# A planner's duration for leaving narrow products, and a new order from it, in a linear attention and MoE kernel

## The chip, the cores and the metric

One Trainium2 chip, one core of it. The metric is the device time of one execution in microseconds (us). The kernel before took 662.56 us (median of 3 runs, 660.89 to 663.44).

## The reference: what is computed

Two layers, one after the other. The first is a complex-valued linear attention over 4 batches, 8 heads, 768 steps and a head dimension of 48. Each step decays a 48 by 48 state by a normalised complex factor, adds an outer product and reads the state:

```
mag = sqrt(a_re*a_re + a_im*a_im);  scale = min(mag, 0.999) / (mag + 1e-6)
for t in range(S):
    S_re, S_im = ar*S_re - ai*S_im + kv(t), ar*S_im + ai*S_re
    y[:, :, t] = einsum('bhd,bhde->bhe', q[:, :, t], S_re)
```

The second takes y as 3072 tokens of 384 numbers through a two-layer network: `gelu(x @ w_in) @ w_out`, with 2048 hidden units and weights that arrive as 64-bit floats.

## The kernel before, in words

**Lanes.** The decay factors are turned into running products. The sequence is cut into four groups of chunks (GROUPS, two of 64 steps and two of 128, each with a mirrored second half), and each group into 4 or 8 slices of 8 rows. `tick` (line 703) does one slice: it normalises the factors of a later slice, runs the scan of this one (`scan`, line 666: for each row a 192-column multiply and a 96-column add on VectorE, each dependent on the last), and turns keys and queries by the products (`towards`, `against`, line 645). What comes out is stored to a buffer in DRAM (tile kq) and loaded again as kqn by the units. `ending` (line 681) and a last `squares_b` and `logs` close a group. In the profile lanes work is a, tab, bt, tt, xt.

**Weights.** 32 pieces (`weights`, line 502), each a 384 KB load into raw, four VectorE instructions on raw, wh, wi_lo or wo_lo, some ScalarE instructions and three TensorE products that split each weight into a high and a low part (wi_hi, wi_lo, wo_hi, wo_lo).

**Units.** 24 units of 128 tokens (`unit`, line 786). Each loads keys, queries and values, turns keys and queries, makes scores (tile kp), outputs and the update of the state st. Its products of at most 64 output rows are called narrow: att<-kp,vn, att<-qT,st, att<-vn,kqn or att<-vn,raw in the profile. The first eight units hold two chunks, the others one. In the latter the narrow products are made `together`, as one step that nothing can be put into.

**Blocks.** 9 blocks of two or three units (`block`, line 1044). For each of 16 pieces of the hidden dimension a block makes the first product (ph<-xT,wi), Gelu on ScalarE twice, a subtraction on VectorE, and the second product (po<-wo), each as three products of high and low parts.

**The order of all work.** Nothing is issued when these functions run. They only hand steps to a planner (class Plan), which knows for each step its engine or engines, its cost and what it must come after. `natural` (line 274) gives each step a starting rank: the length of the longest path behind it, with the scan's VectorE chain weighted by WL, plus a number for its kind from MORE (lanes0 to lanes3, weights, units, blocks). `forward` (line 292) then plays the program through: on each engine, of the steps that are ready, the one of highest rank goes next; on TensorE a step of the same form as the last is preferred where its rank is within STAY, 1.0, of the best. Where a step can go to more than one engine, it goes where its end plus that engine's BIAS is least. `backward` (line 376) plays the plan from its end, and its times are the ranks of the next `forward`. After PASSES, 4, of these the plan with the shortest estimate is kept (`order`, line 406) and issued (`issue`, line 420). The lines of the profile therefore name the place of issue, line 429, for nearly everything; the tiles tell the work apart.

In `forward` TensorE's form of products (narrow, turn, round, full) costs time at a change, and nothing else depends on it:

```
if e == "tensor":
    if start - free[e] > COLD:
        warm = start + WARM
    if start < warm:
        cost *= 2
    if s.form != form:
        cost += ENTER.get(s.form, 0.0) + LEAVE.get(form, 0.0)
    form = s.form
```

Of the kernel before, what the change touches and what calls it, by code (L numbers as in the profile page):

```python
# [79 lines left out]

ROUND, PASS = 0.462e-3, 0.4219e-3

ENTER, LEAVE = dict(narrow=0.09), dict(narrow=0.2, turn=0.075)
STAY = 1.0
COLD, WARM = 3.0, 4.0
TABLES = {AF.Ln: "natural_log_exp_and_others", AF.Exp: "natural_log_exp_and_others", AF.Gelu: "gelu"}
# [8 lines left out]
EARLIER, N_RAW, N_KP = 1, 4, 2  # L95
PASSES = 4
N_A = 4
WL = 4.532

MORE = dict(lanes0=483.83, lanes1=-1595.06, lanes2=-3639.85, lanes3=-3453.18, weights=-1624.01, units=-66.21, blocks=-85.66)  # L100
BIAS = dict(vector=-0.82, scalar=-1.94, gpsimd=0.93, sync=-6.23)


class Step:
# [8 lines left out]
class Plan:  # L113
# [160 lines left out]
    def natural(self):  # L274
# [4 lines left out]
        for i in range(len(steps) - 1, -1, -1):  # L279
# [9 lines left out]
            rest[i] = t  # L289
        return [t + MORE[s.kind] for t, s in zip(rest, steps)]  # L290

    def forward(self, rank):
# [14 lines left out]
        while len(order) < len(steps):  # L307
            best = None
            for e, waiting in pool.items():
# [8 lines left out]
                if len(steps[i].options) > 1:  # L318
                    ends = {o: max(free[o], ready[i], port[other[o]] if o in steps[i].port else 0.0) + c + BIAS[o] for o, (_, c) in steps[i].options.items()}
                    if ends[e] > min(ends.values()) + 1e-9:  # L320
# [119 lines left out]
def lanes_and_chunks(ctx, tc, flags, a_lanes, x_lanes, v_units, w_in, w_out, out):  # L440
# [650 lines left out]
    def ticks(g):  # L1091
        P.chain["vector"] = "lanes", WL
        with P.work(f"lanes{g}"):
            for s in range(end):
                if slices[s][0] == g:
                    tick(s)
        P.chain.pop("vector")
# [255 lines left out]
```

## Time and profile before

| what | value |
|---|---|
| median of 3 runs | 662.56 us |
| lowest and highest run | 660.89, 663.44 us |
| profiled execution, first to last instruction | 659.6 us |
| the profiled span below the median of the runs | 3.0 us |
| TensorE busy | 614.1 us, 93% |
| VectorE busy | 484.1 us, 73% |
| ScalarE busy | 434.1 us, 66% |
| GpSimd busy | 26.1 us, 4% |
| granted TensorE clock, mean | 0.973 |

The profile has one execution, whose span is given from its first to its last instruction; a time of its own beside the span is not given, so the span is set against the median of the runs, 3.0 us above it. In the rows, PE is TensorE, PEld its loading of weights, DVE VectorE, ACT ScalarE, POOL GpSimd and SPq the queue of SyncE, which issues the transfers. A product of two 32-bit operands is two instructions of PE, so counts of such products are twice those of the code. A start-to-start time in the timeline is the time that a run of instructions took up; the second number in a row is its duration, which overlaps the next.

### The profile page before, as it was taken

The numbers are of one execution on the slowest core, as the hardware profiler recorded it, in microseconds if no ns is written. First come the engines' busy times: TensorE is split into PE (matmuls) and PEld (weight loads), VectorE is DVE, ScalarE is ACT, GpSimd is POOL, SyncE is SP. The second block draws the span as 40 slices with busy tenths as digits, with TensorE's granted clock in tenths as the row PEclk, the third lists the DMA queues.
The fourth block names the chain that finished last, engine by engine and source line by source line (L and its number), as shares of the span: only waits on it lengthen the run. The fifth ranks groups of instructions, "written<-read, shape, count | busy, mean of one in ns | idle before, by whom it ended". The sixth has DMA issues, their size and how long they took to land.

```text
span 659.6 us, 13997 instructions
## 1 busy us (share of the span) xinstructions
PE 614.1 (93%) x5154; PEld 563.8 (85%) x5154; DVE 484.1 (73%) x1204; ACT 434.1 (66%) x1107; POOL 26.1 (4%) x74
## 2 busy tenths in 40 slices
PE   4655499999999999999999999999999999999995
PEld 2322277988789999999999999999999999999995
DVE  6999999999999999999989999656334424232211
ACT  8976699999998979787476997535442422232332
POOL 1000100002000000120000000020000000000000
PEclk9787699999999999999999999999999999999999
DMA  9366876668266456687889966487444132110000
GB/s 322 119 158 161 256 225 212 185 196 258 71 197 173 116 135 177 163 173 158 198 198 219 230 157 166 116 167 169 104 88 88 50 64 46 34 51 15 25 1 27
DMA packets 210442, 93.51 MB, mean 142 GB/s; under 512 B 167744, under 2 KB 202688, under 8 KB 210368
## 3 DMA queue, kind: packets, MB, share of 16 engines
q1 hardware_dynamic: 210368, 92.57, 54.6%
q8 instruction: 41, 0.67, 0.4%
q14 instruction: 33, 0.27, 0.1%
HBM read 63.11 MB, written 25.69 MB: 135 GB/s over the span
## 4 chain that ended last, share of the span: by engine, by line
PE 70%; ACT 9%; DVE 9%; issue 2%; DMA 1%; SPq 0%; DVEq 0%; ACTq 0%
PE po L429 27%; PE ph L429 26%; PE att L429 17%; DVE a L429 2%; ACT a L429 1%; DVE tt L429 1%; ACT tab L429 1%; ACT L429 1%; ACT L427 1%; DVE xt L429 1%; ACT gh L429 1%; DVE bt L429 1%; ACT gf L429 1%; DMA raw<-in_w_pieces_dram 1%; ACT square L429 1%
## 5 line engine op out<-in xcount | busy, mean ns | idle before, releaser
L429 PE MATMUL ph<-xT,wi_hi 128*128 128x384 f32 (+1 forms) x864 | 209.2, 324 | 0.0
L429 DVE TENSOR_TENSOR gl<-gf,gh 128x384 fp32r<-128x384 f32 (+1 forms) x144 | 73.7, 512 | 126.4 <-ACT gf L429 126.0
L429 ACT ACTIVATE gh<-ph 128x384 fp32r<-128x384 f32 (+1 forms) x144 | 65.8, 457 | 149.6 <-PE ph L429 149.2
L429 PEld LDWEIGHTS ph<-xT,wi_hi 128*128 128x128 f32 x864 | 154.3, 188 | 2.2 <-ACT gf L429 0.2
L429 PE MATMUL ph<-xT,wi_lo 128*128 128x384 f32 (+1 forms) x432 | 137.3, 318 | 0.0
L429 PE MATMUL po<-wo_hi,gh 128*128 128x384 f32 x384 | 132.5, 345 | 0.9 <-ACT gh L429 0.7
L429 PE MATMUL po<-wo_lo,gh 128*128 128x384 f32 x384 | 129.7, 338 | 0.0
L429 PE MATMUL po<-wo_hi,gl 128*128 128x384 f32 x384 | 92.5, 342 | 0.0
L429 PEld LDWEIGHTS ph<-xT,wi_lo 128*128 128x128 f32 x432 | 81.3, 188 | 0.1
L429 PEld LDWEIGHTS po<-wo_hi,gh 128*128 128x128 f32 x384 | 72.1, 188 | 3.0 <-ACT gh L429 2.0
L429 PEld LDWEIGHTS po<-wo_lo,gh 128*128 128x128 f32 x384 | 72.5, 189 | 0.0
L429 DVE TENSOR_TENSOR tt<-bt,a 128x192 f32<-128x192 f32 x192 | 67.3, 350 | 0.5
L429 PEld LDWEIGHTS po<-wo_hi,gl 128*128 128x128 f32 x384 | 65.9, 188 | 1.6 <-DVE gl L429 0.7
L429 ACT ACTIVATE gf<-ph 128x384 f32<-128x384 f32 (+1 forms) x144 | 65.4, 454 | 2.5 <-DVE gl L429 2.5
L429 DVE TENSOR_TENSOR bt<-tt 128x96 f32<-128x96 f32 x192 | 48.1, 250 | 0.5
L429 PEld LDWEIGHTS att<-qT,kp 96*64 96x64 f32 (+1 forms) x512 | 39.4, 165 | 2.4 <-issue 1.5
L429 PE MATMUL att<-qT,kp 96*64 96x64 f32 (+1 forms) x512 | 41.0, 250 | 0.0
L429 DVE TENSOR_TENSOR kp<-att,causal 128x512 f32<-128x512 f32 x40 | 27.5, 687 | 9.5 <-PE att L429 9.4
L429 ACT ACTIVATE a<-tab 128x384 f32<-128x384 f32 (+1 forms) x48 | 25.6, 534 | 9.3 <-DVE tab L429 9.2
L429 PE MATMUL po<-wh,ident_r 128*128 128x384 f32 x48 | 22.0, 541 | 9.4 <-DVE wh L429 9.3
L429 PE MATMUL att<-tab,ident_r 128*128 128x384 f32 (+1 forms) x20 | 14.8, 896 | 13.6 <-ACT tab L429 13.6
L429 ACT ACT_TABLE_LOAD x21 | 26.9, 1283 | 0.3
(154 smaller groups left out, 992.9 us busy)
## 6 DMA issues: line engine op xcount, KB each, us to landing
kqn<-kq SPq DMA_DIRECT2D x96, 128.0 KB, 3.2
xt<-in_x_lanes_dram SPq DMA_DIRECT2D x24, 384.0 KB, 4.4
kq<-xt SPq DMA_DIRECT2D x48, 192.0 KB, 3.5
a<-in_a_lanes_dram SPq DMA_DIRECT2D x20, 384.0 KB, 3.4
raw<-in_w_pieces_dram SPq DMA_DIRECT2D x16, 384.0 KB, 4.1
raw<-in_moe_w_out_dram SPq DMA_DIRECT2D x16, 384.0 KB, 4.3
vn<-in_v_units_dram SPq DMA_DIRECT2D x24, 256.0 KB, 3.7
kqn<-kq SPq DMA_DIRECT2D x8, 768.0 KB, 5.7
```

The costliest lines, as they stand in the source:

```text
L427: self.nc.scalar.preload_act_table_set(table)
L429: getattr(getattr(self.nc, engine), name)(*args, **kw)
```

## The change

It changes constants of the planner alone: the duration of leaving narrow products, from 0.2 to 0.09 us, the weight WL, the starting ranks MORE and the preferences BIAS. The whole diff:

```
-ENTER, LEAVE = dict(narrow=0.09), dict(narrow=0.2, turn=0.075)
+ENTER, LEAVE = dict(narrow=0.09), dict(narrow=0.09, turn=0.075)
-WL = 4.532
-
-MORE = dict(lanes0=483.83, lanes1=-1595.06, lanes2=-3639.85, lanes3=-3453.18, weights=-1624.01, units=-66.21, blocks=-85.66)
-BIAS = dict(vector=-0.82, scalar=-1.94, gpsimd=0.93, sync=-6.23)
+WL = 4.540
+
+MORE = dict(lanes0=761.48, lanes1=-1519.43, lanes2=-3262.61, lanes3=-8069.14, weights=-1596.23, units=892.75, blocks=-477.53)
+BIAS = dict(vector=-2.11, scalar=-3.87, gpsimd=8.66, sync=-6.23)
```

No step is added or removed; the order of the steps on each engine, and the engine of those that have a choice, come out of the planner anew.

## Rows read from the trace of the kernel before

**Rows 1.** The page: span, busy time, and PE and its granted clock in 40 slices

```profile
span 659.6 us, 13997 instructions
...
PE 614.1 (93%) x5154; PEld 563.8 (85%) x5154; DVE 484.1 (73%) x1204; ACT 434.1 (66%) x1107; POOL 26.1 (4%) x74
...
PE   4655499999999999999999999999999999999995
...
PEclk9787699999999999999999999999999999999999
```

**Rows 2.** Windows: stretch, length, busy us (x instructions) by engine, clock, DMA share, GB/s

```profile
66.00:82.50 16.50, 8.20 (x15) 3.96 (x14) 16.26 (x45) 11.52 (x28) 2.69 (x5) 0.63 0.88 256
...
82.50:260.00 177.50, 176.93 (x2005) 155.52 (x2004) 172.31 (x466) 164.86 (x418) 6.46 (x15) 1.00 0.61 175
260.00:640.00 380.00, 379.56 (x2972) 372.80 (x2971) 235.80 (x533) 200.21 (x518) 13.25 (x26) 1.00 0.52 119
```

**Rows 3.** Groups of DVE from 0 to 60.2 us: the weights' instructions

```profile
L429 DVE SCALAR_TENSOR_TENSOR wh<-raw,wh 128x384 uint32<-128x384 uint32 x10 | 5.5, 554 | 0.1
...
L429 DVE TENSOR_SCALAR wh<-raw 128x384 uint32<-128x384 uint32 x11 | 3.9, 354 | 0.0
L429 DVE TENSOR_SCALAR raw<-wh 128x384 uint32<-128x384 uint32 x10 | 3.6, 357 | 0.1
...
L429 DVE SCALAR_TENSOR_TENSOR wi_lo<-raw 128x384 fp32r<-128x384 uint32 x5 | 2.8, 554 | 0.0
L429 DVE SCALAR_TENSOR_TENSOR wo_lo<-raw 128x384 fp32r<-128x384 uint32 x4 | 2.2, 554 | 0.0
```

**Rows 4.** Timeline of DVE, ACT and SP from 60 to 76 us: start, duration

```profile
60.23 0.25 DVE L429 TENSOR_TENSOR bt<-tt 128x96 f32<-128x96 f32 x1
...
61.17 0.58 ACT L429 ACTIVATE tab<-att,by_partition 128x384 f32<-128x384 f32 x1 [2.67 <-PE att L429]
...
63.26 0.84 ACT L429 ACTIVATE a<-bt 128x768 f32<-128x768 f32 x1
...
70.48 2.62 SPq L429 DMA_DIRECT2D kq<-xt  x3
...
75.78 1.01 SPq L429 DMA_DIRECT2D kqn<-kq  x2
```

**Rows 5.** Timeline of PE around the first narrow runs and around the last

```profile
84.80 1.14 PE L429 MATMUL ph<-vn,kqn 64*64 64x48 f32 x32
85.86 0.75 PE L429 MATMUL att<-ident_r,kqn 128*96 128x128 f32 x8
...
87.61 0.67 PE L429 MATMUL ph<-vn,kqn 64*64 64x48 f32 x16
88.21 0.75 PE L429 MATMUL att<-ident_r,kqn 128*96 128x128 f32 x8
...
599.76 0.34 PE L429 MATMUL po<-wo_hi,gh 128*128 128x384 f32 x1
599.93 0.34 PE L429 MATMUL po<-wo_lo,gh 128*128 128x384 f32 x1
600.20 1.09 PE L429 MATMUL att<-kp,vn 128*64 128x128 f32 x16
...
602.10 0.50 PE L429 MATMUL ph<-xT,wi_hi 128*128 128x256 f32 x2
```

**Rows 6.** Waits of PE's weight loads, 82.5 to 260 us: total us, times, longest

```profile
PEld po L429 <- DVE gl L429: 0.7, 2, 0.6
PEld po L429 <- ACT gh L429: 0.7, 1, 0.7
...
PEld att L429 <- ACT qT L429: 0.5, 1, 0.5
...
PEld att L429 <- ACT kp L429: 0.2, 1, 0.2
```

**Rows 7.** Groups of POOL: the one step on the state

```profile
L429 POOL TENSOR_TENSOR st<-st,m 96x384 f32<-96x384 f32 x1 | 1.0, 1010 | 45.7 <-ACT st L429 45.7
```

## Prediction

> **What bounds the kernel now.** I read the page first, for the span and for the shape of TensorE's (PE's) use: PE is busy for 614.1 us of 659.6, and its slices show two kinds of time, four or five poor slices at the front and a solid row of nines behind [rows 1]. Then the windows by stage. From 66 to 82.5 us PE is busy for 8.20 us of 16.50 at a granted clock of 0.63, which is a mixture of its two levels, 1.2 and 2.4 GHz, after long idle gaps; from 82.5 to 260 us it is busy for 176.93 of 177.50 at full clock, and from 260 to 640 for 379.56 of 380.00 [rows 2]. So the kernel is a prologue of 82.5 us that VectorE (DVE) and ScalarE (ACT) set, and then some 560 us in which PE always has something in hand. In that long part the total of PE's work is fixed, and an order can only change how often PE changes the form of its products and how long it stands between two of them. DVE is busy for 172.31 us of the 177.50 that follow the prologue [rows 2], so in that stretch too whatever DVE does first decides what PE can be given.
>
> The prologue I read in the timeline. The first group of lanes has its last scan step at 60.23 us. Its square on ACT begins at 63.26, because ACT first does work of the second group from 61.17 on; the rows to be stored leave SyncE's (SP's) queue from 70.48, the first unit's load is issued at 75.78 [rows 4], and the first narrow products run at 84.80 [rows 5]. Before 60.2 us DVE also prepares weights: ten pieces, in five groups of instructions whose busy times add up to 5.5 + 3.9 + 3.6 + 2.8 + 2.2 = 18.0 us, so 1.8 us a piece [rows 3].
>
> **The edit to the duration.** It adds and removes no instruction. The number is only added to the planner's own clock when PE goes from narrow products to another form; the choice among ready steps looks at the rank and at STAY, never at this number. In PE's timeline 41 runs of narrow products end, the first at 85.86 us and the last at 602.10 [rows 5], 25 of them before 250 us. What leaving costs the chip can be read there. A run of 32 takes 1.06 us until the next form starts, two runs of 16 take 0.60 each: 2 x 0.60 - 1.06 = 0.14 us for one end more. Entering shows before a run: the step from one 384-column product to the next takes 0.17 us, the one from such a product into a narrow run 0.27, so 0.10 [rows 5]. A visit to narrow products thus costs about 0.24 us beyond its products. The old plan charged 0.09 + 0.20 = 0.29, the new one charges 0.09 + 0.09 = 0.18. **The plan's PE clock goes from 41 x 0.05 = 2.1 us too slow to 41 x 0.06 = 2.5 us too fast** over the whole run, as far as this term goes. I take the edit alone as 0 us on the chip: it moves what the planner believes, by 4.5 us in 660, and is about as far from these rows on the one side as it was on the other.
>
> The row behind this says that a visit has a fixed price that no plan can wish away. The Trainium skill, TensorEngine Tiling (Array Packing), section Tiling Modes, says that changing the tiling mode drains TensorE; by it, an order with more changes would be slower however cheap the planner thinks them, which is the third rival below. The trace bears it out, with its 0.14 us for one more end.
>
> **The new starting ranks (MORE, WL) and preferences (BIAS).** They act on two things. BIAS decides which engine takes a step that two can do. GpSimd's rises by 7.73 and DVE's falls by 1.29, and the one step of this sort that GpSimd has now is a sum of 1.01 us, after ACT's work on the state of a late unit [rows 7]. Moved to DVE, which from 260 us on is busy for only 235.80 us of 380.00 [rows 2], it is hidden by that slack: 0 us, and a few tenths if it stood in the path of a unit. ACT is preferred to DVE by 1.76 where it was 1.12; a copy out of PSUM changing over takes about as long on either, so I give 0 and bound it by 1 us either way, the 1.01 us of the one moved step I can see.
>
> The rest is the order. The first lanes go up by 278, the units by 959, and the blocks down by 392; the third lanes rise by 377 and the last fall by 4616; the rest hardly moves. So of the ready steps a unit's come ahead of a block's, and the first lanes stand further ahead of the weights. The ranks are only where the planner starts: four passes back and forth follow, and the plan with the shortest estimate is kept. What an order can win has two places.
>
> (a) The prologue. Its end moves with whatever lies between 60.23 and 84.80 us. The one plain delay there is ACT's: the square starts at 63.26 though the last row, which begins at 60.23 and takes 0.25 us, was there at 60.48: 2.8 us late [rows 4]. I take half of it, 1.4 us, since another order may as well leave some other small step in front. Bounds: nine us gained (five of the ten pieces put behind the lanes, 5 x 1.8) and 5.4 us lost (three pieces too late for the first block, 3 x 1.8) [rows 3].
>
> (b) The stretch from 82.5 to 260 us. Fifteen rows of waits of PE's weight loads for ACT and DVE run from 0.7 down to 0.2 us and add up to 6.4 us [rows 6]; a part of that is behind products that still run. I take a sixth, 1.1 us, since PE is shown busy for all but 0.57 us there [rows 2]. Bounds: 6.4 us gained if all of it stood open, and 6 us lost if the 25 early visits were doubled (25 x 0.24).
>
> After 260 us nothing is to be won: 0.44 us of PE's time is free [rows 2].
>
> **The sum.** 0 (duration) + 0 (GpSimd's and ACT's steps) - 1.4 (prologue) - 1.1 (stretch behind it) = -2.5 us. Against the profiled execution that is a span of 659.6 - 2.5 = 657.1 us; the median of the runs lies 3.0 us above that span, so the forecast is **660.0 us** against 662.56. Its own range is 656 to 663. It is inside the half per cent (3.3 us) that a measurement of this kernel can tell from no change.
>
> **The rivals.**
>
> Prologue much shorter: half of the early weights go behind the first lanes, so the chain of rows 4 ends 9 us sooner: 653.5 us. For it: DVE has no gaps to hide weights in before 60 us, each of the ten pieces pushes the scan back by its own length, and the lanes' lead over the weights grows by 250. Against it: the lead was some 2100 already and the pieces ran all the same, and PE needs them soon after.
>
> Slower, weights late: with the units ahead of everything else on DVE and ACT, the pieces for the first block arrive after PE has run out of other work. DVE is 97% busy there [rows 2], so it cannot catch up. Three pieces late cost 5.4 us and give 668.0; from two pieces on (3.6 us) it is more than the half per cent. For it: the units' rise of 959 is the largest upward step. Against it: a unit's steps are ready only when its load has landed, and in the meantime weights run.
>
> Slower, more changes of form: the plan believes leaving to be cheap, and mixes narrow runs with other products more finely. The 16 late visits are each issued as one indivisible step; the 25 early ones could double: +6 us, 668.6. It decides from 14 additional visits (14 x 0.24 = 3.4 us). The rule above makes the same point. Against it: the choice does not look at the charge.
>
> Nothing arrives: the order differs only where PE or DVE has cover, and the two planner errors, too slow and too fast, weigh the same: 662.6 us.
>
> **How the numbers follow.** Forecast 0.42, much shorter prologue 0.22, late weights 0.23, more changes 0.05, nothing 0.08. Of the forecast's own range four tenths lie below 659.2, so 0.17 of it counts as faster; with the 0.22 that is 0.39. Slower: 0.20 of late weights and 0.03 of the changes, 0.23. The rest, 0.38, is within 0.5%. The range reaches from 652 to 668: it leaves out the lower part of the first rival (about 0.07) and the upper parts of the two slower ones (about 0.11).
>
> **What would show it.** If (a) holds, the first narrow products start between 80 and 84 us instead of 84.80, and the square that follows the last scan row of the first lanes starts within a microsecond of it. If (b) holds, PE's weight loads wait for ACT and DVE for about 5 us between the prologue and 260 us. The number of narrow runs should stay between 36 and 46, and the GpSimd row of the state should be gone. I am wrong if the start of the first unit moves by more than 5 us either way, if blocks of PE's idle time appear after 90 us, or if the number of visits rises past 55.

## The result, and the profile after

The changed kernel takes 668.83 us (median of 4 runs, 668.44 to 671.93) where the kernel before took 663.00 beside it on the same chip (4 runs). The medians differ by 0.9%; the ratio estimated from all the runs is 1.0101, 95% interval 1.0072 to 1.0130. A second measurement (e5, below) gave the same ratio, 1.0078 to 1.0125. It is 1.0% slower; forecast was 660.0 and a small gain. The profiled execution took 668.44 us, with a span of 666.7 us, 7.1 more than [rows 1]. On the page, PE is busy 4.6 us longer with the same 5154 products, and two slices of the granted clock just behind the prologue are below nine:

```profile
span 666.7 us, 14023 instructions
...
PE 618.7 (93%) x5154; PEld 566.4 (85%) x5154; DVE 483.5 (73%) x1198; ACT 441.8 (66%) x1140; POOL 27.5 (4%) x73
...
PE   4655599999999999899999999999999999999994
...
PEclk9677688999999999999999999999999999999998
```

The windows, with the columns of [rows 2], say in which stretch the time went:

```profile
66.00:82.50 16.50, 9.48 (x19) 4.99 (x19) 16.50 (x46) 10.94 (x25) 5.15 (x7) 0.60 0.77 201
82.50:260.00 177.50, 176.29 (x1984) 154.26 (x1983) 167.99 (x452) 159.25 (x406) 4.91 (x14) 0.97 0.61 174
260.00:640.00 380.00, 377.80 (x2952) 370.56 (x2952) 237.92 (x535) 208.72 (x552) 12.40 (x26) 1.00 0.52 121
```

From 82.5 to 260 us the mean granted clock is 0.97 where it was 1.00, and PE issues 1984 instructions where it issued 2005: the clock rises at 86.7 us instead of 84.1, and falls again for 6.8 us at 97.0. From 260 to 640 us the clock is full, but PE is busy for 377.80 us where it was 379.56: 1.8 us more of standing. What is left is behind PE's last product. That ends at 658.66 + 0.19 = 658.85 us, 7.9 us ahead of the end of the span; before it was 653.50 and 6.1. The last line of PE, before and after:

```profile
653.31 0.19 PE L1284 MATMUL pf<-ones,ok 128*1 128x1 f32 x2 [0.77 <-ACT wh L429]
...
658.66 0.19 PE L1284 MATMUL pf<-ones,ok 128*1 128x1 f32 x2 [0.78 <-ACT wh L429]
```

So three places lose: **the front** (the clock), **the rest** (standing behind 260 us), **the tail** (1.8 us).

The prologue, in the timeline, against [rows 4] and [rows 5]:

```profile
61.43 0.25 DVE L429 TENSOR_TENSOR bt<-tt 128x96 f32<-128x96 f32 x1
...
63.45 0.84 ACT L429 ACTIVATE a<-bt 128x768 f32<-128x768 f32 x1
...
72.14 2.69 SPq L429 DMA_DIRECT2D kq<-xt  x3
...
79.46 1.01 SPq L429 DMA_DIRECT2D kqn<-kq  x2
...
86.48 1.23 PE L429 MATMUL ph<-vn,kqn 64*64 64x48 f32 x32
```

In this pair of profiles the first lanes end 1.2 us later, not sooner, and the first unit starts at 86.48 instead of 84.80. In the groups of DVE up to 61.4 us there are eleven weight pieces ahead of the lanes' end, not the ten of [rows 3].

```profile
L429 DVE SCALAR_TENSOR_TENSOR wh<-raw,wh 128x384 uint32<-128x384 uint32 x11 | 6.1, 552 | 0.1
```

One pair doesn't decide when the lanes end: over all profiles the square on ACT that follows them (63.26 us before, 63.45 after) starts between 61.9 and 64.5 us in the five that begin with the old order (the kernel before, e2, e4, e12, e14) and between 60.8 and 64.8 in the nine that begin with the new one (the changed kernel, e1, e3, e5, e8 to e11, e13). What differs is the way from that square to the first narrow products: 21.5 us in the kernel before, e4 and e12 (23.1 in e14, 23.6 in e2), but 23.0 to 23.1 in seven of the nine with the new order (22.6 in e10, 24.8 in e9). The new order mostly costs 1.5 us there.

What I had listed as signs: 39 runs of narrow products end where 41 did; GpSimd's step on the state is gone; PE's weight loads wait 5.8 us for ACT and DVE between 82.5 and 260 us (15 rows, from 0.9 to 0.2). That is no change: the fifteen rows of the kernel before add up to 5.8 us too (0.7 + 0.7 + 0.6 + 3 x 0.5 + 0.4 + 4 x 0.3 + 4 x 0.2 = 5.9 as printed), not to the prediction's 6.4.

### The profile page after: what moved, and what is told of

Read it like the earlier page. It is cut to its first block, busy times and chain, and to the rows that moved or that the text cites. A ratio compares the mean times of both kernels' runs of the same rounds, so it can differ in the third digit from the quotient of the medians.

```text
span 666.7 us, 14023 instructions
## 1 busy us (share of the span) xinstructions
PE 618.7 (93%) x5154; PEld 566.4 (85%) x5154; DVE 483.5 (73%) x1198; ACT 441.8 (66%) x1140; POOL 27.5 (4%) x73
## 4 chain that ended last, share of the span: by engine, by line
PE 75%; DVE 12%; ACT 7%; issue 2%; DMA 1%; SPq 0%; DVEq 0%; ACTq 0%
PE po L429 29%; PE ph L429 28%; PE att L429 18%; DVE a L429 3%; DVE tt L429 2%; DVE bt L429 1%; ACT a L429 1%; ACT square L429 1%; DVE xt L429 1%; DVE tab L429 1%; DVE wh L429 1%; ACT L429 1%; DMA raw<-in_w_pieces_dram 1%; ACT tab L429 1%; DVE gl L429 1%
## 5 line engine op out<-in xcount | busy, mean ns | idle before, releaser
L429 ACT ACTIVATE st<-st,gg 96x48 f32<-96x48 f32 x112 | 26.7, 328 | 0.9 <-POOL gg L429 0.9
L429 PEld LDWEIGHTS att<-kp,vn 128*64 128x64 f32 (+1 forms) x448 | 20.2, 135 | 6.9 <-issue 3.3
```

Source lines behind the costliest of these rows:

```text
L429: getattr(getattr(self.nc, engine), name)(*args, **kw)
```

## The experiments

My first theory was that the front alone lost, through PE's clock; its rival, that every part of the new order loses a share of its own. In PE's timeline of the changed kernel the first unit's narrow runs come one behind the other, and PE waits once:

```profile
94.00 0.68 PE L429 MATMUL po<-kp,vn 64*64 64x64 f32 x16
95.40 0.67 PE L429 MATMUL ph<-vn,kqn 64*64 64x48 f32 x16 [0.72 <-ACT st L429]
95.90 0.65 PE L429 MATMUL po<-kp,vn 64*64 64x64 f32 x16
96.48 0.69 PE L429 MATMUL po<-qT,st 96*48 96x64 f32 x16
97.11 1.09 PE L429 MATMUL ph<-vn,kqn 64*64 64x48 f32 x16
98.13 1.65 PE L429 MATMUL po<-wh,ident_r 128*128 128x384 f32 x2
```

Sixteen such products take 0.67 us at 95.40 and 1.09 at 97.11: the granted clock has gone to 1.2 GHz, and stays there from 97.0 to 103.8 us. Below I set two profiles against each other by PE's work: both kernels issue the same products, and the delay at a point is by how much later the same sum of full-clock product time has been done.

**e1 and e2, hybrids at the first block.** The plan is made with both sets of constants, and one order follows the other from the first product of a block on (e2 has the two exchanged):

```
+        first, rest = new, old
+        front = first[2][:self.until(first[2], "j0")]
+        final = front + [i for i in rest[2] if i not in set(front)]
```

> Both plans are made in one kernel; what the new plan does before its first block product comes first, then the rest in the old plan's order. Theory (front): the loss is made before the first block, between 94 and 103 us, by PE's clock, which fell to half at 97.0 us for 6.8 us in the changed kernel (3.4 us lost), and a wait of 0.7 us. Then this kernel is 4 to 5 us slower than before, some 667 to 668 us, with a stretch of half clock near 97 us. Rival (everywhere): the new order loses a little all along, because the planner charges too little for leaving narrow products; then this kernel has only a quarter of the loss, 1 to 2 us.

> The other half: the old plan up to its first block product, then the new plan's order. Theory (front): the clock stays full from 84 us on, and only the stall of about 2 us around 270 to 276 us is left, so 0 to 2 us slower than before. Rival (everywhere): 4 to 5 us slower than before.

e1: 666.68 us, ratio 1.0038 (1.0012 to 1.0064). e2: 670.47 us, 1.0102 (1.0065 to 1.0139). e1 lies between its theories. Its profile is its slowest run, 670.57 us: beside the fall at 96.2 us the clock falls once more at 191.8, in the part with the old order, for 6.8 us, and the delay grows there from 4.05 to 8.35 us. e2, with the old front, loses as much as the changed kernel. In e2's profile the delay leaps from 1.0 to 6.3 us between 110 and 122 us, after a wait of PE of 2.68 us from 112.0 on, for ACT's step on a weight piece, and with PE at half clock from 113.6 for 6.8 us. Neither profiled kernel has such a wait there, so I put it down to the cut, at which the two orders have not issued the same steps. e2 doesn't divide the loss.

**e3, full products in the front; e4, the weights' full products taken out of the old front.** e3 issues 16 more products into unused columns of the banks, during the first unit; e4 moves one weight step of the kernel before behind the second unit's scores.

```
+                for _ in range(4):
+                    self.nc.tensor.matmul(out=bank[:, 384:512], lhsT=self.ident[:], rhs=self.ident[:], start=True, stop=True)
```

```
+        late, behind = 358, 731
+        moved, at = [], order.index(behind)
...
+        order = [i for i in order[:at + 1] if i not in moved] + moved + order[at + 1:]
```

> The changed kernel, unaltered in its order, with four added full products of 128 columns ahead of each of the first unit's four narrow steps that follow 88 us of the plan; they write columns that nobody reads. Added work of PE: 16 x 0.11 = 1.8 us at full clock. Theory (front, by the clock): with full products among the narrow ones the clock doesn't fall at 97 us, which gives 3.4 us back; net 1 to 2 us faster than the changed kernel, some 667 us, and the granted clock is 1.00 from 87 us on. Rival (late data: PE waits for DVE and ACT and the clock is a symptom): the added products fall into waits or add to the time; the time is that of the changed kernel or up to 2 us above, and the clock falls all the same.

> The converse in the kernel before: PE's three products of one weight piece, and the copy that takes them, are put some 3 us later, behind the second unit's scores, so that the first units' narrow products stand together for about 9 us as in the changed kernel. Nothing is added. Theory (front, by the clock): the clock falls to half for one stretch between 97 and 105 us and the kernel loses about 3 us. Rival (late data): the clock stays full and the time is that of before within 1 us.

e3: 671.09 us, 1.0097 (1.0062 to 1.0132). The clock is full from 88.3 us on:

```profile
90.00:97.00 7.00, 7.00 (x108) 5.64 (x107) 6.41 (x15) 6.94 (x21) 0.00 (x0) 1.00 0.24 80
97.00:104.00 7.00, 7.00 (x98) 6.07 (x99) 4.69 (x12) 3.14 (x13) 0.00 (x0) 1.00 0.68 164
```

The 16 products are two instructions each, 3.6 us by their durations and not the 1.8 of the expectation; in the timeline they take 4.2 us. Set against the changed kernel, the delay grows between 90 and 105 us by only 0.4 us in spite of them, so some 3.8 us came back: the 3.4 that 6.8 us at half clock cost, and a part of the wait of 0.72 us. For that wait is gone too; the added products fill it (PE busy 7.00 of 7.00 us). e4: 664.66 us, 1.0020 (0.9995 to 1.0045); the clock doesn't fall, and PE waits no more than 0.15 us there before 102 us. So full products held the clock in the profile of e3, and their absence alone didn't bring it down in that of e4, which missed its theory. Whether the clock held in e3 by the kind of the products or because PE no longer stood, these two can't tell apart.

The recorded mean clock of every run goes with the profile of e3: 0.966 to 0.973 in its seven runs, 0.956 to 0.964 in the ten of the changed kernel (the first four and e5). One stretch of 6.8 us at half clock is 0.005 of such a mean. It is the mean of the whole run, though, and doesn't say where.

**e5, the changed kernel again.**

> The changed kernel as it is, for a second profile and more runs. If the fall of PE's clock at 97 us belongs to the order (theory), it is in this profile too, within a few us of that place, and the median is 668 to 670 us. If it was chance (rival), the profile has no fall between 90 and 110 us, and the median comes down to within 2 us of before.

669.23 us, 1.0101 (1.0078 to 1.0125). The clock falls in the same place, at 95.9 us, but for 3.4 us only.

**e6, the duration alone; e7, the other constants alone.**

```
-ENTER, LEAVE = dict(narrow=0.09), dict(narrow=0.2, turn=0.075)
+ENTER, LEAVE = dict(narrow=0.09), dict(narrow=0.09, turn=0.075)
```

e7 keeps the 0.2 and takes the rest of the change's diff.

> Before with the duration of leaving narrow products at 0.09, all other constants as before; the order is planned anew. Theory (the duration is only what starts another order, and each order has its own waits): 3 to 10 us slower than before, by an order as different from both as they are from each other, with PE's waits in other places than in the changed kernel. Rival (the duration itself makes the loss): within 1 us of the changed kernel, with the half clock near 97 us and the wait near 275 us.

> The changed kernel with the duration back at 0.2; starting ranks and preferences are the new ones. Theory: 3 to 10 us slower than before again, by yet another order. Rival (the duration makes the loss): back at the time of before within 1 us.

e6: 672.16 us, 1.0135 (1.0113 to 1.0157). e7: 674.90 us, 1.0171 (1.0147 to 1.0194). Each part alone is slower than both together: e6 by 9.4 us over the kernel before, within its theory's 3 to 10, e7 by 12.2, above it. They lose in other places, and the clock falls there too: in e6 at 186.9 us for 6.8, in e7 at 111.7 for 10.2. The longest of PE's waits in e6 from 150 to 195 us:

```profile
PE att L429 <- DMA kqn<-kq: 2.6, 1, 2.6
```

And the only one in e7 from 104 to 125 us:

```profile
PE att L429 <- ACT qT L429: 2.0, 1, 2.0
```

The stretch of e7 that has this wait and the fall behind it, with the columns of [rows 2]:

```profile
104.00:125.00 21.00, 18.98 (x211) 15.36 (x206) 18.82 (x57) 16.66 (x52) 0.00 (x0) 0.76 0.78 244
```

So it is not that one constant is bad and the other good. Each set makes the planner roll a new order, and of the four orders on record the old one suits the chip best.

**e8, the logarithms one step later.** Behind 260 us the changed kernel's PE waits 0.57 and 1.52 us around ACT's table loads:

```profile
271.01 0.49 ACT L429 ACTIVATE gh<-ph 128x384 fp32r<-128x384 f32 x1
...
272.02 1.28 ACT L427 ACT_TABLE_LOAD   x1
...
274.51 1.28 ACT L429 ACT_TABLE_LOAD   x1
275.80 0.49 ACT L429 ACTIVATE gf<-ph 128x384 f32<-128x384 f32 x1
...
276.35 0.62 PE L429 MATMUL ph<-xT,wi_hi 128*128 128x384 f32 x2 [1.52 <-ACT gf L429]
```

ACT issues the first half of a pair (gh), then loads a table, takes the logarithms of a gate, loads the other table back, and only then the second half (gf) that frees the bank. In the kernel before both halves are ahead of the load:

```profile
266.28 0.50 ACT L429 ACTIVATE gh<-ph 128x384 fp32r<-128x384 f32 x1
...
267.39 0.50 ACT L429 ACTIVATE gf<-ph 128x384 f32<-128x384 f32 x1
...
268.41 1.28 ACT L427 ACT_TABLE_LOAD   x1
```

e8 moves the changed kernel's logarithms behind that gf, by the lines shown for e4 (1278 behind 1660).

> The changed kernel with one step moved on ACT: the two activations with a change of table that stood between two Gelus of one block step at 272 us go behind the second of them. Theory: PE's wait of 1.5 us for that Gelu at 274.5 us goes, and the kernel is 1 to 1.5 us faster than the changed one. Rival (the wait is covered, since PE's products then wait elsewhere): the same time as the changed kernel within 0.5 us, with PE's delay against before, 3.3 us at 250 us, still rising to 5.4 us by 280 us.

668.29 us, 1.0085 (1.0063 to 1.0107), and the wait has moved, not gone; PE's longest from 255 to 300 us is now:

```profile
PE po L437 <- DVE gl L437: 1.6, 1, 1.6
```

By the time e8 lies between the two expectations, 0.9 us below e5, which ran beside it, and the intervals overlap. By the trace the rival holds: against the kernel before the delay still grows by 2.4 us from 250 to 280 us. A single step put right only changed whom PE waits for. Table changes as close to each other (264.23 and 268.41 us) stand in the kernel before without such a wait, so what makes PE short here stays open.

**e9 and e10, the tail.** 13 and 6 loads of 32 bytes on SP's queue, behind 400 us:

```
+                if wait % 12 == 0:
+                    self.nc.sync.dma_start(out=self.spare.pop(), in_=self.some)
```

> The changed kernel with 13 loads of 32 bytes added to SP's queue behind 400 us, into a tile that nobody reads; the output is the reference's. SP's record counts 745 instructions in the kernel before and 732 in the changed one, and after TensorE's last instruction SP stands 1.4 us between two semaphore instructions in the changed kernel and not in the one before. Theory (the longer tail is where the pieces of SP's instruction stream happen to end, nothing that the order does late): with 13 more instructions SP stands as in the kernel before, the time from TensorE's last end to the end of the span falls from 7.9 us to 6.1 to 6.6 us, and the median falls by 1.3 to 1.8 us to about 667.2. Rival 1 (the tail belongs to DVE's stream or to the branch): SP's pause is gone or moved but the tail stays at 7.5 us or more, and the median stays at 668.8. Rival 2 (added loads cost): the tail is over 8 us.

> The changed kernel with 6 such loads on SP's queue instead of 13. Theory (place of SP's stream): SP's pause of 1.4 us moves by about six semaphore instructions towards the front of the row of semaphore instructions that SP issues at the end; the tail stays between 7 and 8 us or falls only as far as the pause comes to lie beside DVE's own pause of 3.3 us behind the branch. Rival (not SP's stream): the pause stays where it was, behind the same semaphore instruction, and the tail at 7.9 us.

SP's instructions in the trace can be counted. Behind its last branch SP issues a row of semaphore instructions, and in the changed kernel it stands 1.40 us between two of them: the branch is its record 710, the pause comes 13 further on. With 6 loads the branch is 716 and a pause of 2.03 us comes 7 further on; with 13 the branch is 723, as in the kernel before, and there is no pause but that of the branch. In the other profiles with a pause of its own it comes at 723 or 724 too. The tail is 6.4 us in e9, as its theory has it, and 8.1 in e10, 0.1 over its range; the place of the pause is as the theory of e10 has it. In the view of SP's waits the changed kernel has one of 3.4 us at the line of the branch, e9 one of 3.0, and e10 two of 5.0 in all, in that order:

```profile
SPq L1287 <- SPq L1287: 3.4, 1, 3.4
...
SPq L1293 <- SPq L1293: 3.0, 1, 3.0
...
SPq L1293 <- SPq L1293: 5.0, 2, 2.9
```

So the longer tail comes from the place at which SP's instruction stream breaks, shifted by the 13 SP instructions that the new order has fewer. One instruction fetch more on the page (34 against 33) doesn't explain it: e9 has 34 and the short tail. The medians did not show it: e9 took 670.50 us, 1.0097 (1.0062 to 1.0132), where its theory has 667.2; the front of its profile is late, as told next. e10's single run took 664.76 us.

**e11, both cures; e12, the kernel before again.**

> The changed kernel with the 13 small loads and with 8 full products of 128 x 128 x 128 in the first unit's narrow runs, half of the 16 of the run before; 16 TensorE instructions of 0.112 us, 1.8 us. Theory (clock and tail are two thirds of the loss): the granted clock stays full from 89 us on, 3 us come back there and 1.8 us are paid for it, the tail is 1.5 us shorter; median 665.5 to 667, last end of TensorE at 657.5 to 659.5. Rival 1 (8 are too few): the clock falls near 96 us as in the changed kernel, the median is 668 to 670. Rival 2 (the loss sits in the order of the later part): the clock stays full, but the later stalls grow by what the front wins, and the median stays at 668 or more.

> The kernel before once more, for a second profile of it. Theory (its order keeps TensorE's clock full, and so its front ends earlier): full clock from 85 us on as in its first profile, last end of TensorE at 652 to 656 us, a tail of 6.1 us. Rival (the fall is chance and strikes either order): a stretch at half clock between 86 and 125 us here too, and a last end of TensorE 2 to 4 us later.

e11: 669.29 us, 1.0098 (1.0069 to 1.0127). The tail is 6.8 us, and the clock holds from 87 us to 158.6, where it falls for 3.4 us behind a wait of PE of 2.09 us for ACT's step on a weight piece; the waits around 270 us are all there. The theory missed: the front wins, and what it wins is lost later, as in the second rival, but in part by the clock. e12: 659.74 us; from 61 us to the end it repeats the first profile with a constant shift of 1.4 us, at full clock from 82.6 us and with a tail of 6.0, as its theory has it.

These two, and e9 and e10, decide what the front is. e10 and e9 differ from the changed kernel only behind 400 us, so up to there they are further samples of the same order. The windows from 90 to 104 us, of the changed kernel:

```profile
90.00:97.00 7.00, 6.28 (x140) 5.12 (x136) 5.76 (x14) 6.62 (x21) 0.00 (x0) 1.00 0.25 57
97.00:104.00 7.00, 7.00 (x42) 4.40 (x38) 4.85 (x13) 3.66 (x12) 0.00 (x0) 0.51 0.97 280
```

The same work in e10, whose first unit starts 3.06 us sooner:

```profile
87.00:94.00 7.00, 6.28 (x140) 5.09 (x136) 5.75 (x13) 6.62 (x21) 0.00 (x0) 1.00 0.31 68
94.00:101.00 7.00, 7.00 (x108) 5.14 (x106) 6.83 (x18) 6.71 (x19) 0.00 (x0) 1.00 0.95 273
```

The kernel before, in e12, from 90 to 104 us:

```profile
90.00:97.00 7.00, 7.00 (x120) 5.62 (x117) 6.03 (x18) 7.00 (x27) 0.00 (x0) 1.00 0.80 203
97.00:104.00 7.00, 7.00 (x108) 5.23 (x106) 6.79 (x20) 6.86 (x23) 0.00 (x0) 1.00 0.73 228
```

The new order leaves PE 0.72 us without work ahead of 97 us, in the changed kernel and, 3 us sooner, in e10 alike, with the same 140 instructions. In the one the clock falls, in the other it does not, and then e10 is 1.5 us ahead of the first profile of the kernel before at 250 us. In e9 the clock comes up only at 94.5 us, and it is 6.3 us behind. Of seven profiles with this front and no added products (the changed kernel, e1, e5, e8, e9, e10, e13) five fall at 95.9 to 97.5 us for 3.4 to 6.8 us, one comes up late, one stays full. Of four with the old front to 250 us (before, e4, e12, e14) none falls there and one, e14, comes up late, at 90.5 us. Both profiles of the kernel before are at its best, though: their mean clock is 0.973, and of its 57 runs beside the experiments one reaches that, the median is 0.966, and the 13 runs from 0.970 on have a median of 661.7 us, the 7 below 0.962 one of 663.9.

Two things in the record say more about the front. First, counted from the square on ACT, which takes out when the lanes end, the delay against the kernel before at 254 us follows the length of the fall: 1.0 us in e10 (no fall), 1.8 in e5 and in e8 (3.4 us at half clock), 3.1 in the changed kernel and in e13 (6.8 us). So some 1 us is the order's own and up to 2 us are the clock's. Second, in all 16 profiles the clock falls eleven times between 86 us and PE's last product, and each time behind a wait of PE of 0.7 to 2.7 us, which ended at most 2.5 us before or still lasted. The reverse doesn't hold: the changed kernel's wait of 1.52 us near 275 us and e6's of 2.60 near 162 have no fall behind them.

**e13 and e14, hybrids at 250 us**, where both orders have issued nearly the same steps (the lines of e1 with "j2"):

> The changed kernel's order up to the first product of the third block stage (about 250 us), the order of the kernel before for the rest. Theory (the front's loss is the clock's and varies, the later loss is the order's): the runs scatter as the front does, between 660 and 668 us, median 663 to 666, of which the kernel before has 662.1; the stall at 264 to 276 us is not there, and no delay is added behind 250 us beyond 1 us. Rival 1 (all of the loss is in the front): median 667 or more. Rival 2 (all of it is behind 250 us): median 660.5 to 662.5, at or below the kernel before.

> The kernel before up to the first product of the third block stage, then the changed kernel's order. Theory: the front repeats the kernel before's, and behind it come 2 to 3 us at the gates' logs; 1.5 us more if SP's pause falls into the tail as in the changed kernel. Median 664.5 to 667, with a last end of TensorE 2 to 3.5 us later than the 652.1 to 653.5 of the kernel before. Rival 1 (all of the loss is in the front): 661.5 to 663. Rival 2 (all of it is behind 250 us): 668 or more.

e13: 665.62 us against 661.76, 1.0057 (1.0030 to 1.0083). e14: 669.02 us, 1.0098 (1.0065 to 1.0131). In e13 the half clock is there at 96.0 for 6.8 us, the delay is 2.55 us at 254 us and 2.51 at the end: nothing more is lost, and its theory holds. The fall is in its window from 97 to 104 us:

```profile
97.00:104.00 7.00, 7.00 (x58) 4.75 (x58) 4.14 (x12) 3.94 (x12) 0.00 (x0) 0.58 0.87 247
```

In e14 the standing around 270 us is that of the changed kernel. PE's waits from 255 to 300 us, in e13:

```profile
PE po L456 <- ACT gh L456: 0.2, 1, 0.2
```

and in e14:

```profile
PE ph L456 <- ACT gf L456: 1.5, 1, 1.5
PE po L456 <- ACT gh L456: 0.6, 1, 0.6
```

The window from 260 to 640 us, in e13:

```profile
260.00:640.00 380.00, 379.56 (x2968) 372.86 (x2967) 237.65 (x537) 202.09 (x521) 13.47 (x27) 1.00 0.52 120
```

and in e14:

```profile
260.00:640.00 380.00, 377.41 (x2943) 369.60 (x2942) 240.08 (x538) 208.39 (x551) 12.40 (x26) 1.00 0.53 122
```

In this window PE is busy 379.54 to 379.57 us in all five profiles with the old rest (before, e1, e4, e12, e13) and 376.73 to 377.80 in all nine with the new one (the changed kernel, e2, e3, e5, e8 to e11, e14). e14's median is above its theory and in the range of its second rival (all of the loss behind 250 us), which e13's loss with the old rest rules out. Its own profile tells why for that run: a front late by 5.2 us at 250 us, though the order there is the old one, 3.0 from the clock that rises late and 2.2 from a wait of 1.76 us for a load at 160 us with 3.4 us at half clock behind it; behind 250 us the delay grows by 2.95 us and the tail is 8.6 us. Its lowest run, 665.74 us, is 5.6 above the lowest of the kernel before, near to 2.95 + 2.5. Why its other runs are higher, and why e9's are, stays open; in e14 it isn't the mean clock, which is 0.965 at 666.8 and at 670.3 us. By the medians the two halves, 3.9 and 7.3 us, add up to more than the whole, so the shares below are read from the profiles and are approximate.

## Why the prediction was wrong

The step that failed is the sum. It has two terms, both gains, -1.4 and -1.1 us, and what a new order can lose stands in it as nothing: as 0 for the duration, as "nothing is to be won" behind 260 us, and not at all for the clock and the tail. Losses appear only among the rivals, with other mechanisms. The runs showed none of the two gains, and three losses.

The loss of 6 to 7 us has three parts. **The front**: e13 has the new order up to 250 us alone and loses 3.9 us (2.0 to 5.5), of which some 1.06 is its tail; so about 2.8. Its profile has 6.8 us at half clock, which cost 3.4, more than its whole delay of 2.5 us; e10, the same front without the fall, is not late at 250 us. **The rest**: from 254 to 640 us the delay grows by 2.1 us in the changed kernel, 2.9 in e10, 2.95 in e14 and 3.5 in e5, of it 2.1 in two waits at 270 and 276 us. **The tail**: 1.8 to 2.2 us more than before in the four profiles of that order without added loads (the changed kernel, e3, e5, e8). With 2.1 to 2.95 for the rest that is 6.7 to 8.0 us, where the medians of the two measurements differ by 5.8 and 6.5 us and the ratio gives 6.7.

Point by point:

- *The duration as 0 us on the chip.* The price of a visit, 0.24 us, was not tested by any run. But the step that treats the edit as a small error of the plan's clock failed: alone it costs 9 us (e6), since it makes another order, and orders differ by more than the whole error of 4.5 us. The reason given, that the choice never looks at this number, is wrong by the code: `forward` adds it to `cost` and so to `free[e]`, up to which a step has to be ready to be chosen from, and `backward` makes the next ranks of `cost`. So it isn't true of the planner that nothing else depends on it.
- *(a) Prologue, -1.4.* Wrong in sign. I read the raised rank of the first lanes as lanes ahead of weights; the profile has one piece more ahead of them (eleven against ten). The square does follow its last row sooner, 63.45 - 61.68 = 1.8 us behind it instead of 2.8, but behind the square the first unit comes 1.5 us later in most profiles. The first narrow products start between 83.42 and 89.18 us in five profiles of the new front (the changed kernel, e5, e8 to e10), mean 86.05, and between 83.36 and 86.03 in four of the old, mean 84.96: +1.1, which alone would not be clear of that scatter.
- *(b) 82.5 to 260 us, -1.1.* The term rests on a wrong sum, 6.4 us for rows that add up to 5.8, and the waits did not shrink: 5.8 us after. In e10, where the clock held, the delay at 250 us against the kernel before is -1.5 in one pair of profiles and about 0 in the other. What I left out is the clock: [rows 2] show 0.63 in the prologue and 1.00 behind, and I took the 1.00 as given to the stretch, not to the order. 6.8 us at half clock cost 3.4, and that stood nowhere in my sum.
- *"After 260 us nothing is to be won."* True, and I took it for "nothing can happen". With 0.44 us free, a new order can win next to nothing there and lose more, and it lost 2 to 3.
- *The tail.* Not in the sum at all; 1.8 us in the first profile.
- *GpSimd's and ACT's steps, 0.* Not tried apart, so no run shows it.
- *The rivals.* The late weights came within 1 us of the time (668.0), by luck, since the mechanism is another: no row shows PE waiting long for a weight piece in that stretch (the only one is 0.3 us); it waits for ACT's state, 0.72 us, and then runs at half clock. Long waits for a weight piece are there in e2 and e11 alone (2.68 and 2.09 us). More changes of form did not happen, the visits went down. The Trainium skill, TensorEngine Tiling (Array Packing), section Tiling Modes, with its drain at a change of mode, is neither confirmed nor contradicted by a loss with 39 visits instead of 41.
- *What would show it.* Of my three signs of being wrong two did not come (first unit off by over 5 us, over 55 visits), and blocks of idle time came only small, 0.72, 0.57 and 1.52 us, where the kernel before has none over 0.47. The forecast was wrong all the same: the signs watched for the mechanisms that I had thought of.

What stays open: what decides whether the clock falls near 96 us. PE's busy share ahead of it is the same 6.28 of 7.00 us, over the same 140 instructions, with a fall and without. The Trainium skill, TensorE: Matmul & The Clock Gate, section Part 1: The HAM clock gate, says that the clock follows how busy PE has lately been; the full products of e3 agree, but by the busy time of those 7 us alone the changed kernel and e10 should have fared alike. That the wait of 0.72 us brings the fall about was not tried by removing the wait alone: e3 takes it away, but together with a change of the products around it.

## What to carry to other kernels

When a planner's constant is edited, the object that changes is the order, and a new order is a new draw: cost it as such, with the scatter that other re-plans show (here +1.0, +1.35 and +1.7%, three draws, from an order already chosen), and not by the size of the constant's error. In a kernel whose main engine has 0.4 us free in 380, look for where an order can lose: waits around table loads, a front that barely holds the clock, the end. To divide a loss between stages, cut the two orders together where both have issued the same steps (e13 with 250 us), not where one is ahead (e1 and e2 with 110 us).

## What the runs showed of the hardware

PE, busy for 6.28 of the 7.00 us ahead, lost its full clock for 3.4 or 6.8 us at the same place of the order in five of seven profiles. Every fall behind the prologue came behind a wait of PE of 0.7 to 2.7 us, and waits as long stayed without one. The kernel before, run 57 times beside the experiments, lies between 659.7 and 667.1 us, though its two profiles run in step, 1.4 us apart, from 61 us to the end. And SP stops for 1.3 to 2.1 us at one count of its recorded instructions, 723 or 724, in eleven profiles; in the other five its last branch, which pauses anyhow, falls on that place. The tail is 7.0 to 8.6 us in the eleven and 6.0 to 6.8 in the five.
